# Hedgehog linear attention and a ReGLU feed-forward on one core: engine orders from a table, finer first loads, part of the first v scaling on VectorE

## The chip, the core and the metric

The kernel runs on one core of a Trainium2 chip. The metric is device time in microseconds (us) of one execution, as the median of several. The engines are TensorE (PE in the profile; its weight loads are PEld), VectorE (DVE), ScalarE (ACT), GpSimd (POOL) and SyncE (SP), which only issues transfers here.

## The reference, cut to what matters

```python
# q, k, v: (8, 8, 576, 64) f32; w_phi: (64, 128); w_gate, w_val: (512, 1536); w_out: (1536, 512)
def phi(x):
    proj = einsum('bhsd,df->bhsf', x, w_phi)
    proj = proj - max(abs(proj), axis=-1, keepdims=True)
    return concatenate([exp(proj), exp(-proj)], axis=-1)
q_p, k_p = phi(q), phi(k)
kv  = einsum('bhsf,bhsd->bhfd', k_p, v)
z   = sum(k_p, axis=2)
num = einsum('bhsf,bhfd->bhsd', q_p, kv)
den = einsum('bhsf,bhf->bhs', q_p, z)[..., None] + 1e-06
x   = (num / den).transpose(0, 2, 1, 3).reshape(4608, 512)
out = (maximum(x @ w_gate, 0) * (x @ w_val)) @ w_out      # 4608 x 512 f32
```

The kernel works through eight batches. Of each, 512 positions form one feed-forward group; the remaining 64 positions of all batches together form a ninth.

## The kernel before

Work is written down as operations (`op`) with an estimated duration, dependencies, buffers and PSUM banks. Nothing is emitted at that point. A list scheduler then plays the operations through its own clock, always taking the ready operation with the best key, and the result is the instruction order of every engine. The orders are fixed when the kernel is built; at run time every engine executes its own list strictly in order and waits where a semaphore says so.

```python
def run(self, quota):                       # the scheduler of before, cut
    ...
    while left:
        now = heapq.heappop(events)
        for e in wait:                      # each engine that is free now
            best = None
            for o in wait[e]:               # best ready operation by key
                ...
            if best is None:
                if e == PE and self.WARM[0] <= now < self.WARM[1]:
                    ...                     # a zero matmul keeps TensorE busy
                continue
            ...                             # give it buffers, banks, a time
```

The scaling of v by the k factors, the item that the change touches:

```python
def scale(eng):                                    # one pair of heads
    eng.tensor_tensor(vs.t[:, :, :, 0:D],
        vn.t[:, 2*u : 2*u+2]...to_broadcast([P, 2*C, 2, D]),
        e.t[:, :, :, None].to_broadcast([P, 2*C, 2, D]), op=ALU.mult)
    eng.tensor_copy(vs.t[:, :, :, D], e.t)
engs = (POOL, DVE) if dve_scale else (POOL,)       # dve_scale is False
```

First loads and the second batch's, which stand behind the scalings in GpSimd's queue:

```python
k_heads = ((0, 2), (2, 4), (4, 8))
heads_of(0, "vn", v, SP, 0, 4, (0, 4)); heads_of(0, "vn", v, SP, 4, H, (0, 5))
o_first = heads_of(0, "qn", q, POOL, 0, H, (0, 10), [last_k])
low = (2, 0, 0, 8.7)
heads_of(1, "kn", k, POOL, 0, H, (*low, 0), [o_first])      # k of the second batch
```

The turn (transpose) of the normalised attention output to xT is done on TensorE for the first batch and by a transposing DMA, issued from SP, for all others. Such a DMA and a load are kept apart: each is held until the other kind before it has landed (`o.alone`, `o.gate`).

```python
def q_num(..., pe_turn=False):
    ...
    if not pe_turn:
        return turn_dma(flat, dst, P * DM * 2, dst_buf, [o_x], key, xu)
    ...                                             # four TensorE transposes and a copy
# first batch: pe_turn=True; the others: pe_turn left False
```

The first group's feed-forward comes in two parts of 256 columns, `parts = [(0, SF//2, xo[0:2]), (SF//2, SF, xo[2:4])]`.

Of the kernel before, what the change touches and what calls it, by code (L numbers as in the profile page):

```python
# [18 lines left out]
class Buf:  # L19


    __slots__ = ("ring", "slot", "users", "free_at", "lock", "by", "place")

    def __init__(self, ring):
        self.ring, self.slot, self.users, self.free_at, self.lock = ring, None, 0, 0.0, 0.0
        self.place, self.by = ring.made, None
        ring.made += 1
# [6 lines left out]
class Ring:  # L34
    def __init__(self, name, tiles):
        self.name, self.tiles = name, tiles
        self.free = {i: 0.0 for i in range(len(tiles))}
        self.made = self.taken = 0
# [18 lines left out]
class Plan:  # L57


    RATE = {POOL: 320.0, SP: 290.0}  # L60
    LAT = {PE: 0.26, ACT: 0.16, DVE: 0.2, POOL: 0.15, SP: 0.1}
    SAME = {PE: 0.0, ACT: 0.1, DVE: 0.1, POOL: 0.15, SP: 0.1}
    MARGIN = 0.2
    COLD = 5.5
    SWITCH = 0.06
    WARM = (1.3, 24.0)
    STICK = 1.0
    PAD = 2.0

# [3 lines left out]
    def op(self, eng, dur, fn, deps=(), bufs=(), banks=(), key=(9,), kind="", nbytes=0, pad=0.0):  # L73
        o = Op(eng, dur, fn, [d for d in deps if d is not None], list(bufs), list(banks), key,
               kind, nbytes, pad)
        o.n = len(self.ops)
        self.ops.append(o)
        for b in (*o.bufs, *o.banks):
            b.users += 1
        return o  # L80

    def rank(self, batches):

        for o in self.ops:
            o.left = len(o.deps)
            for d in o.deps:
                d.succ.append(o)
        for n, part in enumerate(batches):
            own = set(map(id, part))
            for o in reversed(part):  # L90
                after = max((s.tail for s in o.succ if id(s) in own), default=o.tail)
                o.tail = o.bias + after + min(o.dur.values()) + self.LAT[o.eng[0]] + o.pad
                if o.bytes:
                    o.tail += 2.3 + o.bytes / 3e5
                o.key = (2, n, -o.tail)

    def run(self, quota):
        wait = {e: [] for e in (PE, DVE, ACT, SP, POOL)}
        free = dict.fromkeys(wait, 0.75)
        free[POOL] = 0.25  # L100
        held = {}
        dma_free = {}
        last_load = last_turn = None
        mode = 0

        def release(o):
            for e in o.eng:
                wait[e].append(o)

        for o in self.ops:  # L110
            if not o.left:
                release(o)
        now, left = 0.0, len(self.ops)
        events = [0.0, 0.25, 0.75, self.WARM[0]]
        order = []
        while left:
            if not events:
                stuck = [(o.kind, o.key, o.eng) for w in wait.values() for o in w]
                raise RuntimeError(f"stuck at {now}: {len(order)} done; {stuck[:12]}")
            now = heapq.heappop(events)  # L120
            while events and events[0] <= now + 1e-9:
                heapq.heappop(events)
            progress = True
            while progress:
                progress = False
                for e in wait:
                    if free[e] > now + 1e-9:
                        continue
                    best = None
                    for o in wait[e]:  # L130
                        key = o.key
                        if e == PE and o.mode and o.mode == mode:
                            key = (*key[:2], key[2] - self.STICK)
                        if o.start is not None or (best and key >= best_key):
                            continue
                        r = o.ready.get(e, 0.0)
                        if e == PE and o.kind[0] == "a":
                            r += self.MARGIN
                        if r > now + 1e-9:
                            heapq.heappush(events, r)  # L140
                            continue
                        if any(b.lock > now + 1e-9 and b.by != e for b in o.banks):
                            continue
                        if o.alone:
                            t = dma_free.get(POOL if e == SP else SP, 0.0)
                            if t > now + 1e-9:
                                heapq.heappush(events, t)
                                continue
                        ok = True
                        need = {}  # L150
                        for b in (*o.banks, *o.bufs):
                            if b.slot is None:
                                need[b.ring] = need.get(b.ring, 0) + 1
                        for b in o.bufs:
                            if b.slot is None and b.place >= b.ring.taken + need[b.ring]:
                                ok = False
                        for ring, n in need.items():
                            if sum(t <= now + 1e-9 for t in ring.free.values()) < n:
                                ok = False
                        if ok and o.banks and o.banks[0].slot is None:  # L160
                            k = o.kind[0]
                            if held.get(k, 0) >= quota(k, now):
                                ok = False
                        if ok:
                            best, best_key = o, key
                    if best is None:
                        if e == PE and self.WARM[0] <= now < self.WARM[1]:
                            free[e] = now + 0.11
                            heapq.heappush(events, free[e])
                            w = Op(PE, 0.11, self.warm, [], [], [], (99,), "w", 0, 0.0)  # L170
                            w.start, w.end, w.land = now, free[e], free[e]
                            order.append((now, len(order), w, e))
                        continue
                    o = best
                    progress = True
                    left -= 1
                    for b in (*o.banks, *o.bufs):
                        if b.slot is None:
                            ring = b.ring
                            b.slot = min(  # L180
                                (i for i, t in ring.free.items() if t <= now + 1e-9),
                                key=lambda i: (ring.free[i], i),
                            )
                            del ring.free[b.slot]
                            ring.taken += 1
                            if b in o.banks:
                                held[o.kind[0]] = held.get(o.kind[0], 0) + 1
                    d = o.dur[e]
                    if e == PE:
                        if o.mode != mode:  # L190
                            d += self.SWITCH
                        mode = o.mode
                        if now < self.COLD:
                            d *= 1.8
                    o.start, o.end = now, now + d
                    free[e] = o.end
                    o.land = o.end + self.LAT[e]
                    o.land += o.pad
                    if o.alone and e == SP:
                        o.gate, last_turn = last_load, o  # L200
                    if o.alone and e == POOL:
                        o.gate, last_turn = last_turn, None
                    if o.bytes and e == POOL:
                        last_load = o
                    if o.bytes:
                        begin = max(o.start + 1.3, dma_free.get(e, 0.0))
                        dma_free[e] = begin + o.bytes / self.RATE[e] / 1e3
                        o.land = dma_free[e] + 1.0 + o.pad
                    order.append((o.start, len(order), o, e))
                    for en in o.eng:  # L210
                        wait[en].remove(o)
                    heapq.heappush(events, o.end)
# [33 lines left out]
    drop = []  # L246
# [3 lines left out]
def kernel(  # L250
# [17 lines left out]
    C = 4  # L268
# [853 lines left out]
    for x in xTs[0][1][:2]:  # L1122
        x.tail = 6.0
# [61 lines left out]
```

## Time and profile before

| | before |
|---|---|
| median of the first three runs (range) | 409.3 us (407.12 to 410.19) |
| span of the profiled run | 406.0 us |
| TensorE busy | 380.2 us, 94% |
| one feed-forward group alone, at the end | 31.07 us (96 matmuls in 20.72, 48 in 10.36) |
| first feed-forward matmul | 35.82 us |
| last matmul to the end | about 4.6 us |

From the page of before: the busy table, then the span in 40 slices of about 10 us with the busy tenths of TensorE and ScalarE and the granted TensorE clock in tenths.

```profile
PE 380.2 (94%) x3264; PEld 208.1 (51%) x3264; DVE 279.3 (69%) x686; ACT 219.8 (54%) x477; POOL 166.3 (41%) x199
...
PE   7868899949999999999789999989999999999995
...
ACT  2976984058829948779472688069712311311310
...
PEclk9996999988999999999999999999999999999999
```

TensorE is the bound over most of the span. The exceptions are the first 50 us, the slices near 90 us and those near 200 us. ScalarE, which should feed TensorE in the start, falls to 6 and 4 tenths near 30 and 60.

The same in stretches of before. Columns: window; its length; then busy us and instructions of PE, PEld, DVE, ACT and POOL; granted clock; mean busy share of the DMA engines; GB/s.

```profile
30.00:40.00 10.00, 8.62 (x104) 6.86 (x104) 7.09 (x22) 6.47 (x14) 2.51 (x3) 0.66 1.31 205
...
80.00:100.00 20.00, 14.88 (x123) 6.72 (x120) 16.80 (x42) 12.44 (x28) 11.73 (x13) 0.83 0.58 115
...
190.00:210.00 20.00, 15.67 (x107) 6.97 (x106) 14.52 (x33) 12.53 (x28) 15.96 (x19) 1.00 0.51 80
```

TensorE's waits in before, from three questions of the waits view: 0 to 60 us (first three lines), 60 to 200, 200 to 330. Columns: engine, output and line that waited, what it waited for, us in total, times, longest.

```profile
PE ps L486 <- DMA kn<-in_k_dram: 3.3, 1, 3.3
PE ps L809 <- POOL xu L796: 1.8, 2, 1.4
...
PE ps L541 <- DMA kT<-kn: 3.3, 2, 2.3
PE ps L588 <- DMA kmT<-km: 2.4, 1, 2.4
PE ps L838 <- DVE mk L552: 1.8, 1, 1.8
...
PE ps L659 <- ACT qp L515: 1.8, 1, 1.8
```

The wait list understates the gap at 80 to 100. The timeline of TensorE in before shows three waits in a row, and the last matmul group then runs at half clock (four matmuls of 512 columns in 1.89 us; at full clock they take 1.03). In square brackets: idle time before, and what ended it.

```profile
84.05 0.40 PE L541 MATMUL ps<-w,kT 64*128 64x128 bf16 x8 [1.03 <-DMA kT<-kn]
...
87.30 0.62 PE L541 MATMUL ps<-w,kT 64*128 64x128 bf16 x16 [2.29 <-DMA kT<-kn]
89.72 1.89 PE L838 MATMUL ps<-xT,wv_sb 128*128 128x512 bf16 x4 [1.80 <-DVE mk L552]
```

What held those transposes can be read from SP's queue, in order of issue (timeline of SP in before):

```profile
44.53 1.30 SPq L502 DMA_TRANSPOSE qmT<-qm  x1
74.61 0.37 SPq L884 DMA_DIRECT2D out_dram<-ob  x1
76.31 2.50 SPq L502 DMA_TRANSPOSE xT<-xu  x2
...
87.27 1.22 SPq L502 DMA_TRANSPOSE xT<-xu  x1
```

SP issues nothing from 45.8 to 74.6: a store stood in its queue and waited 28.7 us for the output copy. All turns of the second batch's xT and of the third batch's k lie behind it, and the last xT turn is issued at 87.27. The matmul at 89.72, the first to read an xT after that, starts 2.45 us later. The waits view puts its wait down to the maximum mk, which came last by the profile; I read it as the turn's. The timeline of the weight loads says so too (the load ahead of that matmul waited 1.97 us for the turn of xT).

For a finer account I added up, from the matmul counts of the timeline, the useful time of TensorE (each matmul at its unstalled time of this trace: 0.2158 us for 512 columns, and so on) and subtracted it from the time. The "loss" so counted falls by about 0.36 us per 10 us of pure feed-forward, because a matmul that straddles the edge of a 10 us window was counted in both windows. Counted once each from the packed trace, the loss of before stays flat there (38.8 at 300, 39.0 at 350).

| loss in us by | 50 | 70 | 100 | 190 | 210 | 300 | 350 |
|---|---|---|---|---|---|---|---|
| before | 23.1 | 23.3 | 30.0 | 26.4 | 30.1 | 29.1 | 27.3 |

### The profile page before, as it was taken

The numbers are of one execution on the slowest core, as the hardware profiler recorded it, in microseconds if no ns is written. First come the engines' busy times: TensorE is split into PE (matmuls) and PEld (weight loads), VectorE is DVE, ScalarE is ACT, GpSimd is POOL, SyncE is SP. The second block draws the span as 40 slices with busy tenths as digits, with TensorE's granted clock in tenths as the row PEclk, the third lists the DMA queues.
The fourth block names the chain that finished last, engine by engine and source line by source line (L and its number), as shares of the span: only waits on it lengthen the run. The fifth ranks groups of instructions, "written<-read, shape, count | busy, mean of one in ns | idle before, by whom it ended". The sixth has DMA issues, their size and how long they took to land.

```text
span 406.0 us, 8662 instructions
## 1 busy us (share of the span) xinstructions
PE 380.2 (94%) x3264; PEld 208.1 (51%) x3264; DVE 279.3 (69%) x686; ACT 219.8 (54%) x477; POOL 166.3 (41%) x199
## 2 busy tenths in 40 slices
PE   7868899949999999999789999989999999999995
PEld 6656588423654555464345536543655444444442
DVE  4877987397778779989677897779767433333432
ACT  2976984058829948779472688069712311311310
POOL 2892946048527924654972279347032000000000
PEclk9996999988999999999999999999999999999999
DMA  7999389781957678679599757780043001002004
GB/s 219 176 198 206 62 138 113 222 157 36 180 129 181 96 179 132 108 141 180 100 100 243 159 83 99 189 182 0 2 79 91 3 26 78 2 26 79 0 6 98
DMA packets 86188, 45.65 MB, mean 112 GB/s; under 512 B 57667, under 2 KB 78787, under 8 KB 86147
## 3 DMA queue, kind: packets, MB, share of 16 engines
q0 software_dynamic: 29312, 20.65, 31.0%
q1 hardware_dynamic: 56834, 24.46, 26.2%
q8 instruction: 25, 0.41, 0.4%
q14 instruction: 17, 0.13, 0.1%
HBM read 37.81 MB, written 9.44 MB: 116 GB/s over the span
## 4 chain that ended last, share of the span: by engine, by line
PE 76%; DVE 7%; ACT 6%; DMA 4%; issue 2%; POOL 2%; SPq 1%; DVEq 0%; ACTq 0%
PE ps L838 41%; PE ps L869 20%; PE ps L635 4%; PE ps L768 4%; ACT kp L515 2%; ACT qp L515 2%; PE ps L659 2%; DMA kn<-in_k_dram 2%; DVE u L783 2%; PE ps L541 2%; DVE mk L552 2%; ACT val L844 1%; POOL vs L567 1%; DVE t L776 1%; PE ps L486 1%
## 5 line engine op out<-in xcount | busy, mean ns | idle before, releaser
L844 ACT CAST val<-ps 128x512 bf16<-128x512 f32 (+1 forms) x120 | 70.2, 590 | 100.1 <-PE ps L838 92.0
L847 DVE SCALAR_TENSOR_TENSOR h<-ps,val 128x512 bf16<-128x512 f32 (+1 forms) x120 | 75.1, 629 | 52.5 <-PE ps L838 46.1
L838 PE MATMUL ps<-xT,wv_sb 128*128 128x512 bf16 (+1 forms) x432 | 101.5, 360 | 2.3 <-DVE mk L552 1.8
L838 PE MATMUL ps<-xT,wg_sb 128*128 128x512 bf16 (+1 forms) x432 | 100.7, 358 | 0.4 <-ACT val L844 0.3
L869 PE MATMUL ps<-wo_sb,h 128*128 128x512 bf16 x432 | 99.4, 379 | 0.0
L515 ACT ACTIVATE kp<-ps 128x512 bf16<-128x512 f32 x128 | 70.0, 635 | 22.9 <-PE ps L541 20.8
L515 ACT ACTIVATE qp<-ps 128x512 bf16<-128x512 f32 x144 | 80.2, 742 | 3.7 <-DVE u L783 2.4
L796 POOL TENSOR_TENSOR xu<-u,r 128x512 bf16<-128x512 f32 x36 | 37.3, 1042 | 107.4 <-DVE r L793 68.7
L567 POOL TENSOR_TENSOR vs<-vn,ek 128x1024 bf16<-128x1024 f32 x32 | 60.9, 1903 | 18.2 <-PE ps L768 5.9
L838 PEld LDWEIGHTS <-wv_sb 128*128 128x128 bf16 x480 | 44.5, 99 | 45.4 <-issue 4.7
L838 PEld LDWEIGHTS <-wg_sb 128*128 128x128 bf16 x480 | 44.9, 99 | 44.0 <-issue 5.2
L869 PEld LDWEIGHTS <-h 128*128 128x128 bf16 x432 | 40.2, 98 | 45.8 <-issue 2.1
L879 DVE COPY ob<-ps 128x512 f32<-128x512 f32 x30 | 20.7, 690 | 35.1 <-PE ps L869 35.0
L552 DVE TENSOR_REDUCE mk<-ps 128x4 f32<-128x512 f32 x64 | 40.7, 670 | 1.0 <-PE ps L541 1.0
L669 DVE TRANSPOSE_TENSOR_REDUCE mq<-ps 128x16 f32<-128x512 f32 x56 | 36.5, 688 | 3.7 <-PE ps L659 3.6
L783 DVE TENSOR_TENSOR u<-ps,t 128x195 f32<-128x195 f32 (+3 forms) x120 | 35.5, 326 | 0.5
L768 PEld LDWEIGHTS <-qp 128*128 128x128 bf16 x640 | 27.8, 99 | 10.3 <-DVE kv L642 0.3
L768 PE MATMUL ps<-kv,qp 128*128 128x65 bf16 x640 | 30.1, 195 | 0.2 <-DVE kv L642 0.2
L776 DVE TENSOR_TENSOR t<-ps,cq 128x195 f32<-128x195 f32 (+1 forms) x84 | 23.6, 327 | 6.3 <-PE ps L768 6.0
L635 PEld LDWEIGHTS <-kp 128*128 128x128 bf16 x512 | 21.2, 98 | 2.7
L635 PE MATMUL ps<-vs,kp 128*128 128x65 bf16 x512 | 21.7, 193 | 0.0
L635 PE MATMUL ps<-vsm,kpm 128*128 128x65 bf16 x128 | 20.2, 193 | 0.0
(89 smaller groups left out, 312.0 us busy)
## 6 DMA issues: line engine op xcount, KB each, us to landing
out_dram<-ob SPq DMA_DIRECT2D x32, 256.0 KB, 2.5
vn<-in_v_dram POOLq DMA_DIRECT2D x6, 1024.0 KB, 9.8
qn<-in_q_dram POOLq DMA_DIRECT2D x8, 512.0 KB, 7.5
kn<-in_k_dram POOLq DMA_DIRECT2D x7, 512.0 KB, 6.2
wo_sb<-in_moe_w_out_dram POOLq DMA_DIRECT2D x1, 1536.0 KB, 13.1
vn<-in_v_dram SPq DMA_DIRECT2D x2, 512.0 KB, 6.2
vn<-in_v_dram SPq DMA_DIRECT2D x1, 1024.0 KB, 5.6
wv_sb<-in_moe_w_val_dram POOLq DMA_DIRECT2D x1, 1024.0 KB, 11.7
```

The lines of the kernel that those rows point to most:

```text
L515: nc.scalar.activation(dst(s), ps.t.rearrange("p (c f) -> p c f", f=f), AF.Exp, scale=sign)
L552: nc.vector.tensor_reduce(m.t.rearrange("p (i x) -> p x i", x=2)[:, x], ps.t.rearrange("p (c f) -> p c f", f=F), axis=AX.X, op=ALU.max, ap ...
L567: eng.tensor_tensor(vs.t[:, :, :, 0:D], vn.t[:, 2 * u : 2 * u + 2].rearrange("p h c d -> p (h c) d")[:, :, None, :] .to_broadcast([P, 2 * ...
L635: nc.tensor.matmul(acc[:, hh, s, :], lhsT=lhsT, rhs=rhs, start=(n == 0), stop=(n == 19))
L669: nc.vector.tensor_reduce(mdst(x), ps.t.rearrange("p (h j t) -> p h j t", j=NQ, t=32), axis=AX.X, op=ALU.max, apply_absolute_value=True, a ...
L768: nc.tensor.matmul(ps.t[:, E * (2 * i + s) : E * (2 * i + s + 1)], lhsT=qp.t[:, s, h, :], rhs=kv_of[b][h // 2][0].t[:, h % 2, s, :],)
L783: nc.vector.tensor_tensor(u.t[rows, lo : lo + n], ab[:, :, 0], t.t[rows, 0:n], op=ALU.add)
L796: eng.tensor_tensor(xu.t, u.t[:, :, 0:D], r.t.to_broadcast([P, H, D]), op=ALU.mult)
L838: nc.tensor.matmul(ps.t[:, 0:n], lhsT=w[:, dc, P * fi : P * fi + P], rhs=xt()[:, dc, lo:hi], start=(dc == 0), stop=(dc == NDC - 1),)
L844: nc.scalar.copy(val.t[:, 0:n], pv.t[:, 0:n])
L847: nc.vector.scalar_tensor_tensor(h.t[:, fi, lo:hi], pg.t[:, 0:n], 0.0, val.t[:, 0:n], op0=ALU.max, op1=ALU.mult,)
L869: nc.tensor.matmul(ps.t, lhsT=h.t[:, fi, P * t : P * t + P], rhs=wo_sb[:, fi, :], start=(fi == 0), stop=(fi == NFC - 1),)
```

## The change

The intent: an order found by a long search off the chip in place of the greedy scheduler's; the engines of the first 20 us fed in smaller pieces; GpSimd, whose scalings delay the second batch's loads, relieved by VectorE. VectorE's scalings read their factors from PSUM.

```diff
-    def run(self, quota): ...            # the list scheduler, 170 lines
+    def read(self, table):
+        for entry in table.split():
+            if entry[0] == "w":          # so many zero matmuls on TensorE
+                order += [(self.warm, PE)] * int(entry[1:]); continue
+            n, letter, slots = re.fullmatch(r"(\d+)([A-Z])(\w*)", entry).groups()
+            o, e = self.ops[int(n)], LETTERS[letter]     # operation, engine
+            ...                                          # slots: buffers and banks
+ORDER = """0G 3D 9S 4D 1S 8S 11S 10S 5G 7S 6D w21 34P00 15S0 35D w3 32P1 ..."""  # about 130 lines

-    k_heads = ((0, 2), (2, 4), (4, 8))
+    k_heads = ((0, 2), (2, 4), (4, 6), (6, 8))
     # v of the first batch: four pieces for two; q in two; w_gate and w_val in three for two

+    def e_home(name, n, own_port):
+        if own_port:                     # the factors live in a PSUM bank
+            ps = bank()
+            return (lambda: ps.t[:, 0 : 2 * n].rearrange("p (c s) -> p c s", s=2)), ([ps], [])
+        b_ = buf(name)
+        return (lambda: b_.t), ([], [b_])
-    engs = (POOL, DVE) if dve_scale else (POOL,)
+    op(DVE if own_port else POOL, ...)   # own_port: last head pair and the rest, first batch only

+                    pe_turn=b < TURNS,   # TURNS is 2: the second batch's xT on TensorE too
+            if b < TURNS: t_qm = turn_pe(...)            # and its qm
-            parts = [(0, SF // 2, xo[0:2]), (SF // 2, SF, xo[2:4])]
+            parts = [(0, P, xo[0:1]), (P, 2 * P, xo[1:2]), (2 * P, SF, xo[2:4])]
```

In the table's order the second batch's k is issued ahead of most scalings, 24 kv copies and 10 output copies move from VectorE to ScalarE, and the zero matmuls fall from 115 to 87.

## The prediction

> **What bounds it now.** TensorE. Of the 406.0 us span the busy table gives it 94%, VectorE 69%, ScalarE 54%, GpSimd 41%. The chain of waits shows the floor: alone at the end, one feed-forward group takes 31.1 us (96 matmuls in 20.72, 48 in 10.36); nine take 280. Attention matmuls at their unstalled pace in the timeline (20 in 0.61 us, 16 in 0.51) add about 83. So about 363 us are work, 43 lost (my sums):
> - About 23 us in the first 50: the first feed-forward matmul starts at 35.8. Saturated, ScalarE issues an exponential every 0.50 us: 17 us for the first batch's 34, as much again for the second. It also idles about 6 us between 28 and 37, mostly because the second batch's k load is issued only at 23.4, behind GpSimd's scaling of v (four at 1.90 plus 0.25 us, two halves at 1.04 plus 0.21), and lands at 30.6.
> - About 7 us between 80 and 100: TensorE stands behind kT and xT transposes by DMA and the maxima on VectorE, then runs at half clock.
> - About 4 us between 190 and 205 (kmT by DMA 2.4, exponentials 1.8).
> - 4.6 us for the last copy and store.
>
> Half clock after idle (granted 0.50 at 30-34 and 90-94) agrees with the Trainium skill, "TensorE: Matmul & The Clock Gate", Part 1: a window of about 3.4 us idle halves the clock.
>
> **What changes.** No matmul work goes away. The first group's feed-forward comes in 128, 128 and 256 columns: 12 more copies on ScalarE and 12 more products on VectorE, but small ones. ScalarE takes 24 kv and 10 output copies from VectorE, about 16 us, mostly where it has slack. One of four first v scalings and both halves of the rest go to VectorE: 4.7 us off GpSimd, 2.5-3 onto VectorE (estimate from 0.35 us for 195 elements, 0.69 for 512). Their factors lie in PSUM: by "SBUF — State Buffer", Who interferes with whom, one SBUF input keeps VectorE off the port shared with GpSimd; I expect GpSimd's 1.90 unchanged. The second batch's k is issued before the scalings; its xT turns on TensorE instead of by DMA.
>
> **What that is worth.** Start: little. Added up in the new order, the second batch's numerators need 44 us of ScalarE after 29 us of real TensorE work. ScalarE gets going at about 8, so TensorE is then some 23 us behind, as before; ScalarE is merely kept full, about 6 us further on. I give 0-3 us. Middle: that head start and the TensorE turns should close most of the 80-100 gap (5-7 us) and part of the 190-205 one (2-3). New stalls of a tight static order cost 1-3. End: unchanged. Together 9-12 us off, from 409.3.
>
> **Prediction: 397.5 us; 8 in 10 between 390 and 404.5.** Faster by over 2%: 0.73; within 2%: 0.24; slower: 0.03.
>
> **What would show it.** TensorE's waits on DMA transposes at 80-100 and the second half clock gone; ScalarE full from 10 to 50; first feed-forward matmul still at 33-37; the 31.1 us group unchanged; tail 4-5 us.
>
> **What would make it wrong.** The loads may be the real limit of the start (about 200 GB/s for 40 us): reordered, they could help more or stall the finer feed-forward. One late transpose stops an engine in order. If the start loses under 18 us, the result is nearer 390.

## The result, and the profile after

| | before | after |
|---|---|---|
| median (range), 4 fast runs each | 408.85 us (407.12 to 410.19) | 392.36 us (390.28 to 393.32) |
| span of the profiled run | 406.0 us | 391.5 us |
| first feed-forward matmul | 35.82 us | 36.02 us |
| last matmul to the end | about 4.6 us | about 5.85 us |

The ratio is 0.9592, with a 95% interval of 0.9537 to 0.9647. All ratios here are the mean time of one kernel's fast runs over that of the other's fast runs of the same rounds, so they are not quite the ratio of the medians. The kernel before moves by a per cent (medians of its fast runs from 407.22 to 410.33), so times are compared with that in mind.

The page of after, the same four lines:

```profile
PE 375.6 (96%) x3352; PEld 211.1 (54%) x3352; DVE 268.7 (69%) x673; ACT 234.5 (60%) x525; POOL 167.7 (43%) x199
...
PE   7897999999999999999999999999999999999994
...
ACT  3999984379728966595787467954976212212211
...
PEclk9997999999999999999999999999999999999998
```

The dips of TensorE near 90 and 200 us are gone, and ScalarE is at 9 tenths from 10 to 50. The same stretches of after, in the columns explained above:

```profile
30.00:40.00 10.00, 8.18 (x92) 6.76 (x90) 9.13 (x30) 8.97 (x24) 6.66 (x9) 0.67 1.23 240
...
80.00:100.00 20.00, 19.55 (x139) 9.01 (x137) 15.70 (x32) 18.93 (x42) 12.22 (x17) 1.00 0.91 177
...
190.00:210.00 20.00, 19.92 (x135) 9.03 (x132) 16.42 (x37) 17.30 (x39) 14.43 (x17) 1.00 0.88 177
```

TensorE's waits in after, for 0 to 60 us (the largest two), 60 to 200 and 200 to 330:

```profile
PE ps L323 <- DMA wo_sb<-in_k_dram: 1.7, 2, 1.4
PE ps L323 <- DMA qn<-in_q_dram: 1.3, 1, 1.3
...
PE ps L480 <- POOL vs L420: 0.9, 2, 0.5
...
PE ps L480 <- POOL vsm L460: 0.7, 1, 0.7
```

From 60 us on, these lists name no matmul that waits for a transposing DMA, though six batches are still turned that way.

| loss in us by | 50 | 70 | 100 | 190 | 210 | 300 | 350 |
|---|---|---|---|---|---|---|---|
| before | 23.1 | 23.3 | 30.0 | 26.4 | 30.1 | 29.1 | 27.3 |
| after | 20.9 | 20.9 | 19.0 | 15.8 | 14.7 | 10.7 | 9.4 |
| before less after | 2.3 | 2.4 | 10.9 | 10.6 | 15.4 | 18.4 | 17.9 |

The last row tells where the time came from: 2.4 us in the start, 8.5 between 70 and 100, 4.8 between 190 and 210, 3.0 between 210 and 300. Against that stand 1.3 us of added work on TensorE, a tail that is 1.2 us longer, and about 0.5 us by which the count drifts over the difference of the spans. That leaves 14.9; the spans differ by 14.5. The recount with each matmul counted once gives 1.9, 7.9, 5.1 and 2.5 us for the same four stretches and leaves 14.7: the same picture, to about half a microsecond a stretch.

The tail of after, from its timeline. The last copy waits until a store has freed the output buffer, of which there are two.

```profile
382.25 0.69 DVE L722 COPY ob<-ps 128x512 f32<-128x512 f32 x1 [4.09 <-PE ps L712]
...
385.29 0.59 ACT L722 COPY ob<-ps 128x512 f32<-128x512 f32 x1 [3.28 <-DMA out_dram<-ob]
386.68 0.59 ACT L722 COPY ob<-ps 128x512 f32<-128x512 f32 x1 [0.80 <-DMA out_dram<-ob]
```

In before the last copy waited for the last matmul alone:

```profile
401.38 0.69 DVE L879 COPY ob<-ps 128x512 f32<-128x512 f32 x1 [1.90 <-PE ps L869]
```

### The profile page after: what moved, and what is told of

The parts are those of the page before. It is cut to its first block, busy times and chain, and to the rows that moved or that the text cites. A ratio compares the mean times of both kernels' runs of the same rounds, so it can differ in the third digit from the quotient of the medians.

```text
span 391.5 us, 8741 instructions
## 1 busy us (share of the span) xinstructions
PE 375.6 (96%) x3352; PEld 211.1 (54%) x3352; DVE 268.7 (69%) x673; ACT 234.5 (60%) x525; POOL 167.7 (43%) x199
## 4 chain that ended last, share of the span: by engine, by line
PE 55%; DMA 4%; POOL 4%; issue 3%; ACT 1%; SPq 1%; DVE 1%; POOLq 0%; ACTq 0%
PE ps L682 32%; PE ps L712 14%; PE ps L613 3%; PE ps L480 3%; POOL vs L413 2%; DMA vn<-in_v_dram 2%; PE ps L387 1%; DMA kmT<-km 1%; POOL vsm L454 1%; PE ps L504 1%; DMA xT<-xu 1%; DMA out_dram<-ob 1%; DMA vm<-in_v_dram 1%; PE ps L552 0%; ACT kp L352 0%
## 5 line engine op out<-in xcount | busy, mean ns | idle before, releaser
L688 ACT CAST val<-ps 128x512 bf16<-128x512 f32 (+2 forms) x132 | 65.9, 520 | 100.4 <-PE ps L682 96.6
L691 DVE SCALAR_TENSOR_TENSOR h<-ps,val 128x512 bf16<-128x512 f32 (+2 forms) x132 | 74.7, 583 | 46.3 <-PE ps L682 40.3
L712 PE MATMUL ps<-wo_sb,h 128*128 128x512 bf16 x432 | 103.7, 379 | 0.0
L682 PE MATMUL ps<-xT,wg_sb 128*128 128x512 bf16 (+2 forms) x480 | 99.2, 338 | 0.1
L682 PE MATMUL ps<-xT,wv_sb 128*128 128x512 bf16 (+2 forms) x480 | 97.9, 340 | 0.4 <-ACT xT L661 0.2
L682 PEld LDWEIGHTS <-wv_sb 128*128 128x128 bf16 x528 | 46.7, 99 | 40.0 <-issue 1.7
L613 PEld LDWEIGHTS <-qp 128*128 128x128 bf16 x640 | 30.0, 99 | 14.2 <-issue 2.0
L621 DVE TENSOR_TENSOR t<-ps,cq 128x195 f32<-128x195 f32 (+1 forms) x84 | 26.0, 328 | 15.9 <-PE ps L613 9.8
L613 PE MATMUL ps<-kv,qp 128*128 128x65 bf16 x640 | 33.5, 195 | 0.8 <-DVE u L628 0.5
L722 DVE COPY ob<-ps 128x512 f32<-128x512 f32 x20 | 13.6, 680 | 17.8 <-PE ps L712 16.5
L480 PE MATMUL ps<-vs,kp 128*128 128x65 bf16 x512 | 23.3, 193 | 1.3 <-POOL vs L420 0.9
```

The lines of the kernel that those rows point to most:

```text
L480: nc.tensor.matmul(acc[:, hh, s, :], lhsT=lhsT, rhs=rhs, start=(n == 0), stop=(n == 19))
L613: nc.tensor.matmul(ps.t[:, E * (2 * i + s): E * (2 * i + s + 1)], lhsT=qp.t[:, s, h, :], rhs=kv_of[b][h // 2][0].t[:, h % 2, s, :],)
L682: nc.tensor.matmul(ps.t[:, 0:n], lhsT=w[:, dc, P * fi : P * fi + P], rhs=xt()[:, dc, lo:hi], start=(dc == 0), stop=(dc == NDC - 1),)
L688: nc.scalar.copy(val.t[:, 0:n], pv.t[:, 0:n])
L691: nc.vector.scalar_tensor_tensor(h.t[:, fi, lo:hi], pg.t[:, 0:n], 0.0, val.t[:, 0:n], op0=ALU.max, op1=ALU.mult,)
L712: nc.tensor.matmul(ps.t, lhsT=h.t[:, fi, P * t : P * t + P], rhs=wo_sb[:, fi, :], start=(fi == 0), stop=(fi == NFC - 1),)
```

## The experiments

Two theories stood against each other. The first, mine: the gain is made of named waits (the second batch's turns by DMA, the idle ScalarE in the start), so parts of the change, put into the kernel before, should bring most of it. The rival: the gain is the order as a whole, and the parts are worth little in the greedy order. A second question was what bounds the start that remains: ScalarE, VectorE, GpSimd's scaling or the clock. All kernels gave correct results. Ranges are those of fast runs.

| kernel | median (range), us | ratio to before [95%] | profiled span | loss by 70 | loss by 350 |
|---|---|---|---|---|---|
| before | 408.85 | 1 | 406.0 | 23.3 | 27.3 |
| after | 392.36 (390.28 to 393.32) | 0.9592 [0.9537, 0.9647] | 391.5 | 20.9 | 9.4 |
| before_peturn | 404.51 (403.75 to 406.80) | 0.9934 [0.9844, 1.0023] | 402.0 | 23.7 | 22.3 |
| before_k1early | 408.15 (403.54 to 409.40) | 0.9993 [0.9882, 1.0104] | 407.6 | 26.6 | 29.1 |
| greedy_all | 405.57 (403.97 to 407.37) | 0.9952 [0.9859, 1.0044] | 405.6 | 26.7 | 25.5 |
| after_dmaturn | 408.34 (407.46 to 410.49) | 1.0026 [0.9938, 1.0115] | 406.7 | 20.7 | 24.9 |
| after_dmaturn_nogate | 402.30 (401.31 to 403.26) | 0.9874 [0.9804, 0.9945] | slow run | | |
| after_act8 | 396.85 (396.47 to 399.40) | 0.9741 [0.9689, 0.9792] | 397.3 | 25.1 | 16.0 |
| after_dve8 | 396.20 (394.79 to 397.51) | 0.9727 [0.9675, 0.9778] | 393.7 | 23.8 | 10.5 |
| after_pool | 396.32 (396.01 to 398.56) | 0.9742 [0.9692, 0.9793] | 394.3 | 24.6 | 12.8 |
| after_sbuf | 394.53 (392.76 to 396.03) | 0.9685 [0.9632, 0.9737] | 393.0 | 23.7 | 10.0 |
| after_fill | 390.68 (390.47 to 392.09) | 0.9597 [0.9539, 0.9655] | 390.2 | 20.3 | 7.6 |
| after_ends | 391.70 (389.62 to 392.04) | 0.9603 [0.9551, 0.9655] | 390.1 | 21.6 | 8.9 |
| after_best | 390.01 (389.18 to 390.89) | 0.9508 [0.9471, 0.9545] | 387.7 | 18.3 | 6.4 |

The four kernels from before_peturn to after_dmaturn shared a chip on which the kernel before was unusually scattered (405.26 to 414.11 us, three of its seven runs slow), hence their wide intervals; there the traces carry the argument. A profiled run is one run: the spans of after's own four runs range from 388.4 to 391.5, so differences of a microsecond or two between two profiles are not settled by them. The start moves as much: in the nine profiles whose program is the same up to the first exponential (after and its variants but after_ends), that exponential begins between 7.05 us (after_best) and 9.18 us (after_act8; 8.35 in after). The first 128-column matmuls, too, run at half pace (one every 0.107 us instead of 0.056) until 12.9 us in after but only until 4.2 us in after_best, although the page shows a full clock there: the trace has no clock record for that stretch.

### The second batch's turns on TensorE, in the kernel before

```diff
+                    pe_turn=b < TURNS,
+            if b < TURNS: t_qm = turn_pe(qmf, ...)
```

> The kernel before, with one part of the change alone: the second batch's xT and its part of the mix are turned on TensorE instead of by DMA; the order is still the greedy one. Theory A (the gap at 80-100 us came from turns by DMA, which stand in the store queue behind output stores and behind the landing of the third batch's loads): that gap shrinks, 4 to 7 us faster than before, near 403. Theory B (the order as a whole closed the gap; the place of the turns matters little): within 2 us of before, TensorE again idle 5 us or more between 75 and 105.

The gap at 80 to 100 closed: TensorE shows no wait between 60 and 120, and the loss by 100 is 22.4 us against 30.0. Taking the turns off SP's queue is thus enough to close that gap. It is not the only way: before_k1early, the next run, keeps the DMA turns, its last xT turn is issued as late as in before (86.93 us), and yet in its other order TensorE waits 1.3 us once between 60 and 110 and otherwise at most 0.2 (timeline of SP, then the waits view):

```profile
86.93 1.22 SPq L502 DMA_TRANSPOSE xT<-xu  x1
...
PE ps L541 <- DMA kT<-kn: 1.3, 1, 1.3
```

By the recount it loses 2.1 us from 70 to 100, where before loses 7.4. So in these runs a late turn costs only where the order leaves TensorE nothing else to do. The median of before_peturn (404.51 against 407.22 for the fast runs of before) has an interval that includes no change. And the greedy scheduler orders everything after it anew, and between 240 and 262 waits came up that before did not have (waits of TensorE from 230 to 270):

```profile
PE ps L635 <- POOL vsm L614: 1.8, 2, 1.0
PE ps L588 <- DMA kmT<-km: 1.8, 1, 1.8
```

The loss grew from 20.3 at 210 to 24.0 at 300. Of 7.6 us that the part brought at 100, some 5 remained at 350, less 1.1 us of added transposes: the span is 4.0 shorter.

### The second batch's k issued earlier, in the kernel before

```diff
-    heads_of(1, "kn", k, POOL, 0, H, (*low, 0), [o_first])
+    heads_of(1, "kn", k, POOL, 0, H, (0, 10.5), [o_first])
```

> The kernel before with the second batch's k load issued on the GpSimd queue between the first scalings of v (about 17 us) instead of after them (23.4 us). If the late k load cost the start its time: TensorE's wait of 3.3 us on it goes, the half clock at 30-37 too, 2 to 4 us faster. If ScalarE's work bounds the start: under 1.5 us faster.

The theory that this one load costs the start fell. ScalarE was busier between 20 and 40 (18.1 us for 14.5), but TensorE then waited 3.3 us for the xT copy on ScalarE and 2.0 us for the km load, and the loss by 50 was 26.4 us for 23.1. The half clock did not go either, as was expected if the load were the cause: it was granted for 13.7 us between 30 and 51 (30.1 to 33.6, 37.0 to 43.8, 47.2 to 50.6), against 6.8 in before. An earlier load in an otherwise greedy order moved the wait elsewhere; since the scheduler ordered everything after the load anew, the load alone was not tested.

### All parts of the change except the table

> All parts of the change except the table: finer loads, scalings on VectorE with factors in PSUM, TensorE turns, first feed-forward in three column parts, ordered by the greedy list scheduler of the kernel before. If the parts carry the gain: 392 to 397. If the table's order carries it: 400 to 408. I expect about 400, half and half.

This is the scheduler of before with the finer loads and feed-forward parts, VectorE's scalings with factors in PSUM, and the turns on TensorE (a few dependencies that only guide the scheduler stay as they were). The edit is the diff shown above without `read` and `ORDER`. The start got worse, 26.7 us lost by 70 against 23.3; from 70 to 350 it lost 5.2 us less than before. The largest waits, first 0 to 60 us, then from 60 on:

```profile
PE ps L486 <- DMA qn<-in_q_dram: 4.6, 3, 2.6
...
PE ps L597 <- DMA kmT<-km: 3.6, 2, 2.4
```

So the parts alone gave some 2 us (405.57 against 407.22 for the fast runs of before, an interval that contains no change), and the order in the table gave the rest: 13 us by medians, 3.6% or 14 to 15 us by the ratios (0.9952 and 0.9592), as the two were not timed in one call. By the loss counts it is about 6 us in the start and about 10 between 70 and 350, which is more than the medians show, as after's tail is longer and both are single profiles. The rival was right about the larger share; the expectation of about 400, half and half, was not met.

### The second batch's turns by DMA again, in the kernel after

```diff
-                    pe_turn=b < TURNS,
+                    pe_turn=False,
-306P51 ... 307A     319P6 ... 320D     332P2 ... 333D     345P2 ... 346A
+306S1               319S               332S               345S
```

> The changed kernel with its table, but the second batch's xT turned by DMA at the same places of the order (four transposes instead of 16 TensorE transposes and 4 copies). Theory A: the turns wait for loads to land, and TensorE, in order, stands for 3 us or more around 60-85: 3 to 8 us slower than the changed kernel. Theory B (order): within 2 us of it.

One part taken out of the finished order cost all of the gain, 16 us, twice what theory A allowed. The start is untouched (20.7 lost by 70), and then one matmul waits 10.7 us:

```profile
85.04 1.89 PE L685 MATMUL ps<-xT,wv_sb 128*128 128x512 bf16 x4 [10.72 <-DMA xT<-xu]
```

SP's waits between 55 and 92 us tell why: each turn stands behind loads which the program does not let it overlap.

```profile
SPq L339 <- DMA wg_sb<-in_moe_w_gate_dram: 49.1, 1, 49.1
SPq L339 <- DMA kn<-in_k_dram: 9.7, 1, 9.7
```

The four turns were issued over 23.3 us, from 60.47 on, and the next batch's kT turn after them. That mixes two costs, the turn by DMA and the gate to the loads, so the next run removed the gate.

### The same without the gate to the loads

```diff
+            o.alone = False        # for the second batch's four turns only
```

> As the run with the second batch's xT turned by DMA, but these four turns no longer wait for loads under way to land (in that run the store queue stood on loads for 49, 10 and 8 us, and TensorE 10.7 us on xT). If the rule that keeps turns and loads apart is what cost the time: within 3 us of the changed kernel (392.4). If a turn by DMA is itself too slow here, each 2.5 us to land and one after the other: still 5 us or more slower. It may give a wrong result if turns must not run beside loads.

The three fast runs gave a median of 402.30 us and a ratio of 0.9874, about 1.5% below the gated version and 2.8% above after. The result was correct here, which is no proof that the gate can be dropped. The profiled run was slow (span 410.0, clock 0.925), so its lengths are not compared; it shows where TensorE waited, 4.4 us for the turn of xT and 4.3 us for an output copy. The gate was thus around a third of the 16 us (6 us by the medians and by the ratios), the turn by DMA in this order the rest: the second theory's result, still 5 us or more slower. I had no run that separates the turn's latency from SP's order.

### Which engine bounds the start

Four kernels on one chip, each with the table of after (in after_pool with GpSimd's letter at the three scalings). Two add work without changing the result:

```diff
+  for _ in range(2 if key[:3] == (2, 1, 0) and sign > 0 else 1):   # after_act8
       nc.scalar.activation(dst(s), ..., AF.Exp, scale=sign)
+  for _ in range(2 if key[:3] == (2, 1, 0) else 1):                # after_dve8
       nc.vector.tensor_reduce(m.t..., op=ALU.max, apply_absolute_value=True)
```

> The changed kernel, with 8 exponentials of the second batch's k (about 30 to 46 us in the trace) done twice: 8 x 0.50 = 4.0 us more ScalarE work, nothing else. If ScalarE's work bounds the first 50 us: 3 to 4 us slower than the changed kernel (395 to 397 against 392.4). If loads, latencies or TensorE bound it: under 1 us slower.

> The changed kernel, with 8 maxima of the second batch's k done twice on VectorE: 8 x 0.58 = 4.6 us more there in the same stretch. If VectorE has slack in the start, as I argued: under 2 us slower than the changed kernel. If VectorE is the tighter of the two: 3 us or more slower.

Eight exponentials more on ScalarE (4.0 us of its time at 0.50 us each) raised the loss by 70 from 20.9 to 25.1, by 4.2 us; the median rose by 4.5. The profiled run was the slowest of the five (399.40; the others 396.47 to 396.87), and its first exponential began 0.8 us later than after's, so some 3.4 us of the 4.2 are left for the added work. Eight maxima more on VectorE (4.6 us) raised it by 2.9, and the median by 3.8. I had expected slack on VectorE and under 2 us; 3 us or more means that VectorE is the tighter of the two. The windows show that either engine, given more work, becomes the full one and the other falls back (after_act8, then after_dve8; in after VectorE is busy 9.13 and ScalarE 8.97 us here):

```profile
30.00:40.00 10.00, 5.56 (x68) 4.08 (x64) 7.58 (x25) 9.66 (x21) 5.50 (x7) 0.70 1.11 216
...
30.00:40.00 10.00, 6.77 (x76) 5.50 (x77) 9.72 (x27) 7.73 (x20) 4.90 (x7) 0.66 1.07 211
```

So the start is bound by ScalarE and VectorE together, each with little slack; which is the tighter is not shown. The medians of after come from another call; by the ratios the two kernels are 1.5% and 1.35% slower than after, 6.1 and 5.5 us, so only the sizes, not the tenths, are meant.

The other two take the scalings apart:

```diff
-        o_s = op(DVE if own_port else POOL, ...                # after_pool: GpSimd again,
+        o_s = op(POOL, ...                                     # and factors in SBUF
-            ps = bank()                                        # after_sbuf: still VectorE,
-            return (lambda: ps.t[:, 0 : 2 * n]...), ([ps], []) # but factors in SBUF
+            ps, e_sb = bank(), single(f"own_{name}", [P, n, 2], FP32)
+            return (lambda: e_sb), ([ps], [])
```

> The changed kernel with the three scalings that had gone to VectorE back on GpSimd at their places in the order, factors in SBUF. 4.7 us more on GpSimd ahead of its loads and later scalings, about 3 us less on VectorE. If the move carries part of the gain: 2 to 5 us slower than the changed kernel. If it is nothing on this path: within 1 us, or faster by what VectorE is relieved of.

> The changed kernel with the scalings still on VectorE, but their factors in SBUF instead of PSUM, so that both inputs lie in SBUF. If that makes VectorE and GpSimd wait for each other: the VectorE scalings or the GpSimd scalings beside them take over 0.5 us longer than in the changed kernel, and the start shifts by 1 to 3 us. If not: same durations, within 1 us.

With the three scalings back on GpSimd, the window from 20 to 30 us of after_pool reads (columns as above):

```profile
20.00:30.00 10.00, 6.77 (x110) 4.96 (x110) 2.87 (x6) 5.69 (x15) 9.98 (x13) 0.84 0.61 67
```

GpSimd is full, VectorE at 2.87 and ScalarE at 5.69 of 10 us: both starve behind it. The loss by 70 was 3.7 us higher than in after. With VectorE doing the scaling from SBUF factors it was 2.8 us higher, so most of what the move to VectorE brought hung on PSUM (by the ratios 3.8 of 6.1 us, by the medians 2.2 of 4.0). The timelines show it. In after, VectorE and GpSimd scale side by side:

```profile
20.47 1.22 DVE L413 TENSOR_TENSOR vs<-vn,ps 128x1024 bf16<-128x1024 f32 x1
20.50 1.93 POOL L413 TENSOR_TENSOR vs<-vn,ek 128x1024 bf16<-128x1024 f32 x1
```

In after_sbuf the same pair takes turns:

```profile
21.10 1.90 POOL L413 TENSOR_TENSOR vs<-vn,ek 128x1024 bf16<-128x1024 f32 x1 [1.38 <-DVE own_ek L364]
21.11 2.97 DVE L413 TENSOR_TENSOR vs<-vn,own_ek 128x1024 bf16<-128x1024 f32 x1
22.95 1.24 POOL L420 CAST vs<-ek 128x16 bf16<-128x16 f32 x1
```

VectorE's 2.97 us are 1.22 of its own and 1.75 of standing behind GpSimd's scaling; GpSimd's small copy then takes 1.24 us for 0.25 while VectorE works. Two inputs in SBUF are not slower by themselves: the scaling of 64x512 in after_sbuf, at a time when GpSimd only issues a load, took as long as with PSUM (0.68 and 0.69 in after):

```profile
18.95 0.69 DVE L454 TENSOR_TENSOR vsm<-vm,own_ekm 64x512 bf16<-64x512 f32 x1
```

This is what the Trainium skill, "SBUF — State Buffer", section "Who interferes with whom", states: a VectorE instruction with two SBUF inputs contends with a GpSimd instruction that reads SBUF, whoever issues first holds the shared ports for the whole instruction, and one SBUF input does not contend. Traces agree on all three.

### The half clock at 34 to 40

In after the granted clock is 0.50 from 34 to 40 us, though TensorE waits at most 0.42 us at a time there. after_fill puts 54 zero matmuls into these waits (new table entries such as `v4`, which write into the bank of the next operation before it does).

> The changed kernel with 54 matmuls of zeros placed in TensorE's short waits between about 27 and 37 us, into banks that the next matmul clears. If the half clock granted at 33.5 to 40 us costs the start: that stretch is at full clock and the start loses 1.5 to 3 us less. If ScalarE bounds the start: the clock stays full but under 1 us is gained.

The clock came back, and the matmul count tells how little was missing (window of after_fill):

```profile
30.00:40.00 10.00, 9.05 (x159) 8.12 (x156) 9.64 (x31) 9.62 (x27) 7.03 (x9) 1.00 1.21 238
```

The loss by 50 fell by only 0.6 us. That fits a start bound by ScalarE and VectorE, in which TensorE's half speed is hidden for the most part. The median was 1.7 us lower than after's, but the ratio of 0.9597 is the same as after's 0.9592, so a gain in time is not shown by this run.

### The tail, and k pieces from a second queue

```diff
+    R["ob"].tiles += [...]           # two idle u tiles serve as output buffers
-2070A1 ... 2075A0                    # the last two output copies
+2070A2 ... 2075D3
-    o = load_main(0, "kn", k, SP, ...)
+    o = load_main(0, "kn", k, ACT if i in (0, 2) else SP, ...)
```

> The changed kernel with two small edits. The last two output copies take buffers of their own (idle work tiles) instead of waiting for stores to free the two that there are: the tail from the last matmul to the end falls from 5.9 us to 5.0 or less. And two of the first four k pieces are issued from ScalarE's queue at once instead of one after another on the store queue: the second piece lands about 1 us sooner than at 6.56, and if ScalarE bounds the start, all of it moves by 0.5 to 1 us. Together 1 to 2 us faster than the changed kernel; if the first loads share a bandwidth limit, only the tail's 0.9.

The tail from the last matmul fell from 5.85 to about 5.0 us. The start did not move: the second k piece was transposed at 5.65 us for 6.56, but the matmul after it then waited 0.94 us for the cast of w_phi and began at 7.76 for 7.71. Two things landed at about the same time, and moving one was worth nothing in this one profile; as the start moves by a microsecond between profiles anyway, a gain of 0.5 us would not show.

### A version with both ends

after_best is after_fill with the two output buffers of after_ends, without the k pieces.

> The changed kernel plus the two edits that each gained about a microsecond alone: 54 small zero matmuls in TensorE's short waits of 27 to 37 us, and a buffer of its own for each of the last two output copies. The two act at different ends, so they should add: granted clock 1.00 in the slice 30 to 40, last 48-matmul group starting at about 374.8 as in after_fill, the end after the last matmul about 5.0 instead of 5.85 us; together 1.5 to 2 us off the changed kernel, so 390 to 391 us and a ratio to the kernel before of 0.955 to 0.960. If the two are not independent (the freed start is spent in a wait later, or the store's landing alone sets the end), it stays at the changed kernel's 392.

It gave 390.01 us, 0.9508 of before, in six runs that all lie between 389.18 and 390.89. The clock is 1.00 in 30 to 40, and the copies of the tail wait for TensorE alone:

```profile
380.22 0.59 ACT L732 COPY u<-ps 128x512 f32<-128x512 f32 x1 [1.15 <-PE ps L722]
382.82 0.69 DVE L732 COPY u<-ps 128x512 f32<-128x512 f32 x1 [2.83 <-PE ps L722]
```

It is the fastest version, 4.9% faster than before. The medians put it 2.4 us ahead of after, the ratios 0.9%, with intervals that barely meet; the two were not timed on one chip. Its last stretch of 48 output matmuls begins at 373.06, earlier than the 374.8 that I expected from after_fill, which has the same start. So about 1.7 us of this profile is scatter between runs. It arises largely in the first 15 us: the first exponential began at 7.05 us against 8.44 in after_fill, and after_fill ran at half clock again from 8.6 to 12.1 us, this run not.

## Why the prediction was right or wrong

The prediction said 397.5 us and a range of 390 to 404.5. The median was 392.36, inside the range, and faster by over 2%. The gain was 16.5 us where the sum gave 9 to 12. The range allowed for that by another route than the one that was taken: it put a result nearer 390 down to a start that loses under 18 us, but the start still lost 20.9 and the surplus came from the middle. That the result lay in the range is in this part luck. Point by point:

- **What bounds the kernel, and where it loses:** held. The losses of before at 50, 80 to 100 and 190 to 210 are where after gained 2.4, 8.5 and 4.8 us.
- **Start, 0 to 3 us; ScalarE merely kept full; first feed-forward matmul at 33 to 37:** held. It gained 2.4 us, ScalarE is busy 9.06, 9.55, 8.97 and 9.85 us in the four tens from 10 to 50 (before: 10.00, 7.98, 6.47, 10.00), and the matmul began at 36.02. The 2.4 us are of the size by which starts differ between profiles; 1.3 of them are there already at the first exponential (8.35 for 9.61). after_act8 and after_dve8 showed the reason for the small gain: ScalarE bounds the start, as said, but VectorE, which I had thought slack, does so nearly as much.
- **Middle, 5 to 7 us at 80 to 100 and 2 to 3 at 190 to 205:** the mechanism was right, the size too small. The terms measured 8.5 and 4.8, and a third, 3.0 us from 210 to 300, was not in my sum. The stretches 100 to 190 and 300 to 350 gave 0.8 back, so 15.5 gross, and less 1.3 us of added TensorE work and 0.5 of the counting some 13.7 net. I had taken the gain to come from "that head start and the TensorE turns". before_peturn shows that moving the turns closes the one gap, before_k1early that another order nearly closes it without; greedy_all shows that all parts together without the table save only 5.2 us from 70 to 350. The step that fell short is to price named parts and to give the order in the table no gain of its own, when it carried some 13 us of the difference; the term so mis-sized is the middle, 5-7 and 2-3 less 1-3 us of stalls, which measured 13.7.
- **"New stalls of a tight static order cost 1-3":** wrong in sign. No stall of over 0.5 us was left from 60 to 200 in after, and one of 0.7 beyond. The stalls came in the greedy orders: every part put into them brought new ones (1.8 to 4.6 us in total for each wait named above). Yet the fear had a ground: after_dmaturn shows that four late transposes in the fixed order cost 16 us, since everything that needs them stands in order behind them.
- **"End: unchanged":** off by 1.2 us. The last copies waited 3.28 and 0.80 us for stores to free the output buffers; after_ends took most of it back.
- **VectorE's scalings, 2.5 to 3 us, GpSimd's unchanged at 1.90:** held. They took 1.22 and twice 0.69 us with the factors in PSUM, GpSimd's 1.91; after_sbuf shows that without PSUM the cost would have been 2.97 for the first.
- **Half clock at 80 to 100 gone:** held, 1.00 for 0.83. At 30 to 40 it stayed (0.67), and after_fill showed that this cost little.

What stays open: which of ScalarE and VectorE is the tighter in the start; how much of the table's 13 us is the order itself and how much its choice of engines and buffers, which the table also holds; and how the 10 us of the ungated turns divide between latency and SP's order.

## What to carry to other kernels

Once the named waits are the last few per cent, the order of a static schedule is a quantity of its own: here nearly the same parts gave some 2 us under a greedy scheduler and 16 in the table's order, so price the order apart from the parts and test both. Double an engine's work in one stretch to learn whether it bounds that stretch, and do so for its neighbours too; here two engines answered alike. Where VectorE multiplies beside GpSimd, try one of VectorE's two inputs in PSUM: it took 1.22 us here for 2.97.

## What the Trainium skill lacked or had wrong

- "TensorE: Matmul & The Clock Gate", Part 1, ties the half clock to an idle window of about 3.4 us. Here it came after less. In before, by the clock records, it began at 30.03, 2.7 us into the wait on a k load, and lasted to 36.9; and it began again at 88.05 after waits of 1.03 and 2.29 us with matmuls between them. In after it came from 33.4 to 40.2 with no recorded wait above 0.42 us between 28 and 42, at 92 small matmuls in 10 us; with 159 it was 1.00. The zero matmuls that make up the difference are plain ones, while 24 of the 92 are transposes, so number and kind are not told apart. The page's section "A second HAM failure mode: psum-queue depth-cycling" speaks of micro-idling, but no page says how dense small matmuls must be to hold the clock.
- "SBUF — State Buffer", "Who interferes with whom", agrees; it gives the rule and slowdowns measured elsewhere, but no shapes or times. Here VectorE's 128x1024 multiplication took 1.22 us with one input in PSUM and 2.97 with both in SBUF beside GpSimd, and GpSimd's 128x16 copy 1.24 for 0.25.
- "DMA: Bandwidth & Descriptors", section "DMA Transpose (X-bar)", lists TensorE as another path for a transpose but not what decides between them in a static order: four turns by DMA gated to loads took 23.3 us to issue and cost 16 us of the median, where 16 transposes on TensorE cost about 0.9 us of it (16 at 0.056).
- I found no page that sizes what the order of a static schedule is worth. Here nearly the same parts took 405.57 us by a greedy list scheduler and 392.36 by the table.
